# A tile's outputs and its state's products put side by side on TensorE, the state's products alternating between a head's halves

## The chip, the cores and the metric

The kernel runs on one NeuronCore of a Trainium2 chip. TensorE (PE, with its weight loads shown apart as PEld) multiplies, VectorE (DVE), ScalarE (ACT) and GpSimd (POOL) work on elements, SyncE (SP) issues most DMA transfers. Each engine takes its own instructions in order and waits for others at semaphores. Tiles lie in the on-chip memory of 128 partitions; TensorE's results go to banks of their own (PSUM), from where VectorE or ScalarE fetch them. The metric is the device time of one execution in microseconds; the median of three runs is given.

## The reference

A linear attention with a complex decay, for 4 batches, 8 heads, 768 steps and 48 columns a head, and then a mixture of 8 experts of which each token takes two:

```python
for t in range(S):
    new_re = ar * S_re - ai * S_im
    new_im = ar * S_im + ai * S_re
    S_re, S_im = (new_re + k_t (x) v_t, new_im)
    y[t] = q_t @ S_re
...
logits = x @ w_gate; noisy = logits + log1p(exp(x @ w_noise)) * noise
out[n] = sum over the best two e of weight * (relu(x @ w1[e]) @ w2[e])
```

Here `ar`, `ai` are the decay's two parts, scaled so that their size stays below 0.999, and x is y with the heads side by side (3072 tokens of 384).

## The kernel before

Attention is done in chunks of 128 steps: 6 groups of 4 tiles, tile n being batch n % 4 and group n // 4. The decay's running products are folded into q and k: `qh` and `kh` hold for each head two halves of 48 columns (the cosine and the sine part, at column 0 and 64). One tile then passes these steps:

- `tr_unit`: 8 transposes of `qh` and 8 of `kh` into the bank pair `ptr` (L298), which ScalarE copies to `qT` and `kT` (L299).
- `sc_unit`, twice, for 4 heads each: scores `psc` (L307), which VectorE multiplies by the causal mask into `am` (L308).
- `st_unit`: the state's products, for each head and each half `kh` times `v`, 48 by 48, into the bank `pG` (L317). The first halves go to partitions 0 to 47, the second to 64 to 111. The loop over the halves is the outer one: eight heads' first halves, then eight heads' second halves. The last group needs none.
- `st_upd`: VectorE adds `pG` to the batch's state `Z` (L326, or copies it in the first group, L329). `st_scale` multiplies `Z` by the chunk's decay (L338).
- `y_unit`: the outputs, 48 rows for each head, in the bank `pY`: `Z` times `qT` (L354, not in the first group) and `v` times `am` (L356), added up. Two heads share a column of the bank, one at partition 0, the other at 64, and the loop goes pair by pair, in turn between the two. ScalarE copies `pY` to `xT` (L357).
- `x_unit`, the gates (`gate_logits`, `gate_dispatch`) and the scatter to the experts' rows follow; part of the first expert's work (`mm1(0, 0)`, into `psc`) is mixed into the last groups.

Two buffers each hold `qh` and `kh` (`NQ` = 2), so that `kh` of tile n+2 (L288) waits until the transposes and the state's products of tile n have read it. `pG` and `pY` are single.

The order of the work is planned. Each step gets a due time from the table `P` by `at(...)`: scores at n - 0.2, state's products at n + 0.05, outputs at n + 0.2, the state's update at n + 0.4. The program is written in the order of these times, and a scheduler then places each instruction on its engine by its own estimate of when operands are ready, by the order of writing, and by a priority (`pri`) that some steps have. It may put instructions of other steps between those of one step. Of each matmul in float32 the trace shows two records.

Of the kernel before, what the change touches and what calls it, by code (L numbers as in the profile page):

```python
# [77 lines left out]
def kernel(  # L78
# [8 lines left out]
    nc = tc.nc  # L87
# [3 lines left out]
    D = HD // H  # L91
# [28 lines left out]
    mask = cp.tile([128, 128], F32, name="mask")  # L120
# [63 lines left out]
    pG = psA.tile([112, H, D], F32, name="pG", bufs=1)  # L184
# [2 lines left out]
    nc.vector.memset(pY, 0.0)  # L187


    RE, IM, T0, TH, TF, TR, EE, QK, V = {}, {}, {}, {}, {}, {}, {}, {}, {}  # L190
    QT, KT, AM, Z, XR, QKD = {}, {}, {}, {}, {}, {}
    XT, FC = {}, {}

    phases = {}

# [6 lines left out]
    def bt(n):  # L202
        return n % B, n // B
# [97 lines left out]
    def sc_unit(n, half):  # L301
        if half == 0:
            AM[n] = pa.tile([128, H, 128], F32, name="am", bufs=2)
        p = psA.tile([128, 4, 128], F32, name="psc")
        for j in range(4):
            h = 4 * half + j
            nc.tensor.matmul(p[:, j, :], KT[n][:, h, :], QT[n][:, h, :], start=True, stop=True)  # L307
        LAST['am'] = nc.vector.tensor_mul(AM[n][:, 4 * half:4 * half + 4, :], p, mask[:, None, :].to_broadcast([128, 4, 128]))  # L308

    def st_unit(n):  # L310
        b, g = bt(n)
        if g + 1 == NG:
            return
        x = kh[n % NQ]
        for r in range(2):
            for h in range(H):
                nc.tensor.matmul(pG[64 * r:64 * r + D, h, :], x[:, h, r, 0:D], V[n][:, h, :], start=True, stop=True)  # L317

    def st_upd(n):
        b, g = bt(n)  # L320
# [19 lines left out]
    def y_unit(n):  # L340

        b, g = bt(n)
        if b == 0:
            XR[g] = pa.tile([128, B, ROW], F32, name="xr", bufs=3)
            nc.gpsimd.memset(XR[g][:, :, RNO + 1:ROW], 0.0)
            nc.gpsimd.tensor_copy(XR[g][:, :, RNO], tokid[:, g])
        XT[n] = pa.tile([128, H // 2, 128], F32, name="xT", bufs=6)
        for i in range(H // 2):
            for z in range(0 if g else 1, 2):
                for r in range(2):  # L350
                    h = 2 * i + r
                    o = pY[64 * r:64 * r + D, i, :]
                    if z == 0:
                        nc.tensor.matmul(o, Z[b][:, h, :], QT[n][:, h, :], start=True, stop=False, skip_group_check=True)  # L354
                    else:
                        nc.tensor.matmul(o, V[n][:, h, :], AM[n][:, h, :], start=not g, stop=True, skip_group_check=True)  # L356
        LAST['y'] = YC[n] = nc.scalar.activation(XT[n], pY, AF.Copy)  # L357


# [75 lines left out]
    def at(step, f, *a):  # L435
        fill.setdefault(step, []).append((f, a))
# [42 lines left out]
        return psA.tile([128, 4, 128], F32, name="psc").rearrange("p a b -> p (a b)")  # L479


    order = mybir.DependencyInfo(mybir.DependencyClass.NoSync, mybir.DependencyReason.DATA)
    LAST = {}

    def behind_of(x, *names):
# [75 lines left out]
    def mm2(e, w):  # L561
        for j in JS[w]:
# [8 lines left out]
            else:  # L571
# [16 lines left out]
    P = dict(la=10, p1=7, d1=1, p2=6, dt=0, ds=0, lqk=6, p3=4, d3=0, q=2, lv=5, xu=0.5, ss=3, gl=0, gd=0.25,  # L588
             tr=1.4, sc=-0.2, st=0.05, y=0.2, up=0.4, w1=16.5, w2=21.1, xt=17.8, m1=18.4, dm=0.36, xu1=22.8, w1b=23, co=6, hg=50,
             hx=50, hl=200, s0=(7, 5.5, 4.5), s1=(7.5, 6, 5), qd=0.05, tk=0.4, sh=0.05)  # L590
    pri = {gdis: P["hg"], x_unit: P["hx"], glog: P["hl"]}
    for g in range(NG):
        f = B * g + .5
        q1, q2, q3 = P.get(f"s{g}", (P["p1"], P["p2"], P["p3"]))
        for j in range(B // 2):
            m = B * g // 2 + j
# [5 lines left out]
        for j in range(B):  # L602
            n = B * g + j
# [5 lines left out]
    for n in range(NT):  # L609
        at(n + .5 - P["lv"], load_v, n)  # L610
        for i in range(2):
            at(n - P["tr"] + P["tk"] * i, tr_unit, n, i)
        for half in range(2):
            at(n + P["sc"] + P["sh"] * half, sc_unit, n, half)
        at(n + P["st"], st_unit, n)
        at(n + P["y"], y_unit, n)
        at(n + P["up"], st_upd, n)
        at(n + .5 + P["xu"], x_unit, n)
        at(n + .5 + P["ss"], st_scale, n)
# [287 lines left out]
```

## Time and profile before

| what | us |
|---|---|
| three runs, median (lowest to highest) | 734.89 (734.31 to 736.23) |
| the profiled execution's span; the page gives no other time of it | 734.8 |
| TensorE, matmuls busy | 696.3 (95%) |
| TensorE, weight loads busy | 620.1 (84%) |
| VectorE busy | 418.7 (57%) |
| ScalarE busy | 329.8 (45%) |
| GpSimd busy | 170.4 (23%) |
| state's products `pG` (L317), 640 records | 31.2, mean 0.210 |
| outputs `pY` (L354 and L356), 704 records | 38.6 + 44.4, mean 0.276 and 0.275 |
| scores `psc` (L307), 384 records | 52.2, mean 0.281 |
| mean granted TensorE clock | 0.993 |

Matmuls overlap in TensorE: a record lasts from its issue until its last result, and the next one starts long before. The time that a series takes is therefore read from the starts, not from the sum of the records. A timeline row holds one or more records of a line that follow each other: start of the first, time until the end of the last, engine, line, operands and count; in brackets the idle time ahead and what ended it.

### The profile page before, as it was taken

To read this page: it belongs to the slowest core of one execution; us is meant where nothing else is said; L and a number is where in the kernel's file an instruction comes from. 1 tells how busy PE (TensorE), PEld (TensorE's weight loads), DVE (VectorE), ACT (ScalarE), POOL (GpSimd) and SP (SyncE) were. 2 spreads that over 40 slices of the span, in tenths; PEclk is the share of its full clock that TensorE was granted. 3 is DMA by queue.
4 is the path that set the end of the run, shared out by engine and by line. 5 is a ranking of instruction groups with operands and counts; after the bars stand their busy time and mean duration, and the time that the engine had idled before them with its cause. 6 is when DMAs were issued, how large, how long until landed. Compare 5 with 4: busy or idle time off the path is not lost.

```text
span 734.8 us, 13448 instructions
## 1 busy us (share of the span) xinstructions
PE 696.3 (95%) x5184; PEld 620.1 (84%) x5184; DVE 418.7 (57%) x946; ACT 329.8 (45%) x545; POOL 170.4 (23%) x187
## 2 busy tenths in 40 slices
PE   1689999999999999999999999999999999999995
PEld 0377687979788979898998999899999899899895
DVE  6788899999987666445255236236227226325321
ACT  6689989797954541333143124125115205203200
POOL 2000003333311254114114124124023123222221
PEclk9989999999999999999999999999999999999998
DMA  7477776754373457126144036028017126212101
GB/s 262 109 240 224 245 205 204 218 163 110 113 204 110 153 169 265 62 93 208 56 160 162 25 121 228 22 75 281 11 65 258 44 68 230 76 37 62 51 28 38
DMA packets 64090, 100.18 MB, mean 136 GB/s; under 512 B 26290, under 2 KB 46363, under 8 KB 64016
## 3 DMA queue, kind: packets, MB, share of 16 engines
q1 hardware_dynamic: 54464, 71.68, 31.2%
q0 software_dynamic: 9552, 27.54, 10.6%
q8 instruction: 43, 0.70, 0.4%
q14 instruction: 31, 0.25, 0.1%
HBM read 68.55 MB, written 32.08 MB: 137 GB/s over the span
## 4 chain that ended last, share of the span: by engine, by line
PE 84%; ACT 5%; DVE 4%; DMA 4%; issue 1%; SPq 1%; POOL 0%; POOLq 0%; ACTq 0%; DVEq 0%
PE po L569 27%; PE ph L545 27%; PE ptr L298 5%; PE psc L307 4%; PE pG L317 3%; PE px L528 2%; PE pY L356 2%; PE cum L251 2%; PE pY L354 2%; PE cum L275 2%; DMA raw<-in_moe_w_dram 2%; PE po L574 2%; PE po L577 2%; PE cum L364 1%; ACT t L200 1%
## 5 line engine op out<-in xcount | busy, mean ns | idle before, releaser
L569 PE MATMUL po<-w2h,h 128*128 128x384 f32 x768 | 198.7, 336 | 0.0
L545 PE MATMUL ph<-x,w1h 128*128 128x512 f32 (+1 forms) x720 | 194.8, 355 | 0.5 <-DVE h L550 0.2
L545 PEld LDWEIGHTS ph<-x,w1h 128*128 128x128 f32 x720 | 127.8, 188 | 16.8 <-issue 0.8
L569 PEld LDWEIGHTS po<-w2h,h 128*128 128x128 f32 x768 | 138.8, 188 | 0.9
L569 PE MATMUL po<-w2l,h 128*128 128x384 f32 x384 | 129.0, 336 | 0.0
L545 PE MATMUL ph<-x,w1l 128*128 128x512 f32 (+1 forms) x360 | 127.6, 355 | 0.0
L550 DVE SCALAR_TENSOR_TENSOR h<-ph,h 128x512 fp32r<-128x512 f32 (+2 forms) x176 | 73.4, 452 | 89.0 <-ACT h L547 88.9
L583 POOL DMA_INDIRECT out_dram<-ao,ox x56 | 54.6, 975 | 287.8 <-DVE ao L582 266.4
L547 ACT ACTIVATE h<-ph 128x512 fp32r<-128x512 f32 (+1 forms) x120 | 61.1, 522 | 116.2 <-PE ph L545 98.0
L421 POOL DMA_INDIRECT xs<-xr,sl x48 | 57.9, 1207 | 208.4 <-ACT t L200 104.7
L582 DVE SCALAR_TENSOR_TENSOR ao<-po,gw,ao 128x384 f32<-128x384 f32 (+1 forms) x56 | 34.2, 613 | 121.0 <-PE po L569 120.9
L545 PEld LDWEIGHTS ph<-x,w1l 128*128 128x128 f32 x360 | 67.7, 188 | 7.9
L569 PEld LDWEIGHTS po<-w2l,h 128*128 128x128 f32 x384 | 72.1, 188 | 0.7
L490 ACT CAST w2h<-raw 128x768 fp32r<-128x768 f32 x32 | 26.7, 836 | 90.7 <-PE po L569 87.1
L556 POOL DMA_INDIRECT ao<-out_dram,ox x49 | 51.7, 1054 | 48.0 <-DMA out_dram<-ao,ox 35.2
L307 PE MATMUL psc<-qT,kT 112*128 112x128 f32 x384 | 52.2, 281 | 0.0
L307 PEld LDWEIGHTS psc<-qT,kT 112*128 112x128 f32 x384 | 48.0, 195 | 2.7 <-issue 1.2
L356 PE MATMUL pY<-am,v 128*48 128x128 f32 x384 | 44.4, 275 | 0.9 <-DVE am L308 0.8
L354 PE MATMUL pY<-qT,z 112*48 112x128 f32 x320 | 38.6, 276 | 0.8 <-ACT xT L357 0.8
L491 DVE TENSOR_TENSOR w2l<-raw,w2h 128x768 fp32r<-128x768 f32 x32 | 30.7, 958 | 13.1 <-ACT w2h L490 11.9
L580 ACT COPY lo<-po 64x384 f32<-64x384 f32 x8 | 3.8, 477 | 73.4 <-PE po L577 73.3
L298 PE MATMUL ptr<-ident,qh 128*112 128x128 f32 x192 | 29.3, 284 | 7.4 <-ACT kT L299 6.7
(209 smaller groups left out, 1010.8 us busy)
## 6 DMA issues: line engine op xcount, KB each, us to landing
raw<-in_moe_w_dram SPq DMA_DIRECT2D x24, 512.0 KB, 4.4
raw<-in_moe_w_dram SPq DMA_DIRECT2D x32, 384.0 KB, 4.1
qk<-in_qk_dram SPq DMA_DIRECT2D x24, 384.0 KB, 3.8
xgb<-xs SPq DMA_DIRECT2D x8, 800.0 KB, 6.2
re<-in_a_dram SPq DMA_DIRECT2D x12, 384.0 KB, 3.4
im<-in_a_dram SPq DMA_DIRECT2D x12, 384.0 KB, 5.5
v<-in_v_dram SPq DMA_DIRECT2D x24, 192.0 KB, 2.5
out_dram<-zero SPq DMA_DIRECT2D x12, 384.0 KB, 5.5
```

The costliest lines, as they stand in the source:

```text
L298: nc.tensor.transpose(p[:, h, :], x[:, h, :, :].rearrange("p r x -> p (r x)")[:, 0:112], ident)
L307: nc.tensor.matmul(p[:, j, :], KT[n][:, h, :], QT[n][:, h, :], start=True, stop=True)
L354: nc.tensor.matmul(o, Z[b][:, h, :], QT[n][:, h, :], start=True, stop=False, skip_group_check=True)
L356: nc.tensor.matmul(o, V[n][:, h, :], AM[n][:, h, :], start=not g, stop=True, skip_group_check=True)
L421: d = nc.gpsimd.indirect_dma_start(out=xs, out_offset=bass.IndirectOffsetOnAxis(ap=sl[:, kk, b:b + 1], axis=0), in_=XR[g][:, lo + b, :], i ...
L545: LAST['m'] = nc.tensor.matmul(p[:, :n], W1[e, kk][i][:, f * 128:(f + 1) * 128], XW[w, kk][:, j, :], start=(m == 0), stop=(m == len(ms) - 1))
L547: nc.scalar.activation(h[:, 0:n], p[:, :n], AF.Relu)
L550: LAST['h'] = nc.vector.scalar_tensor_tensor(h[:, dst:dst + b - a], p[:, a:b], 0.0, h[:, a:b].bitcast(F32), op0=OP.max, op1=OP.subtract)
L556: nc.gpsimd.indirect_dma_start(out=ao[j][0:w, :], out_offset=None, in_=out, in_offset=bass.IndirectOffsetOnAxis(ap=OX[e][0:w, j:j + 1], ax ...
L569: nc.tensor.matmul(p[:, :DM], HT[w, f][i][:, o:o + 128], W2[f // 2][k2][:, f % 2, :], start=(m == 0), stop=(m == len(ms) - 1))
L582: nc.vector.scalar_tensor_tensor(a, p[0:n, :DM], g, a, op0=OP.mult, op1=OP.add)
L583: nc.gpsimd.indirect_dma_start(out=out, out_offset=bass.IndirectOffsetOnAxis(ap=OX[e][0:n, j:j + 1], axis=0), in_=a, in_offset=None, bound ...
```

## The change

In `st_unit` the loops change places: each head's first half is followed by its second. The scheduler gets a high priority (300) for `st_unit` and `y_unit`, and the due time of `st_unit` is now that of `y_unit`, written behind it. Two dependencies are added. The first matmul of the outputs waits for the second half of `am` (with a semaphore, `whole`); before, each waited for the half that it reads, and those that read `Z` for none. The first of the state's products is ordered behind the last of the outputs (`order`, on the same engine and so without a semaphore). What is computed stays the same.

```diff
     def st_unit(n):
         ...
-        for r in range(2):
-            for h in range(H):
-                nc.tensor.matmul(pG[64 * r:64 * r + D, h, :], x[:, h, r, 0:D], V[n][:, h, :], start=True, stop=True)
+        for h in range(H):
+            for r in range(2):
+                m = nc.tensor.matmul(pG[64 * r:64 * r + D, h, :], x[:, h, r, 0:D], V[n][:, h, :], start=True, stop=True)
+                if h + r == 0:
+                    tc.add_manual_dep(m.ins, YL[n].ins.name, order, reason="order")
...
+                    if not started:
+                        tc.add_manual_dep(m.ins, AMD[n].ins.name, whole, reason="whole")
+                    started = True
+        YL[n] = m
...
-    pri = {gdis: P["hg"], x_unit: P["hx"], glog: P["hl"]}
+    pri = {gdis: P["hg"], x_unit: P["hx"], glog: P["hl"], st_unit: 300, y_unit: 300}
...
-        at(n + P["st"], st_unit, n)
         at(n + P["y"], y_unit, n)
+        at(n + P["y"], st_unit, n)
```

TensorE before, tile 7 (`kh_127`, `z_775`; a row is one or more equal instructions, output, inputs, shape of the output), from the last of its scores on:

```order
L307 MATMUL psc<-qT,kT 128x128
L317 MATMUL pG<-v,kh_127 48x48 x2
L364 MATMUL cum<-ident,xT 128x128 x4
L317 MATMUL pG<-v,kh_127 48x48 x2
L298 MATMUL ptr<-ident,kh_126 112x128 x8
L317 MATMUL pG<-v,kh_127 48x48 x12
L354 MATMUL pY<-qT,z_775 48x128 x2
L356 MATMUL pY<-am,v 48x128 x2
```

The same place with the change (lines after the new code have higher numbers: L310 is the scores, L301 the transposes, L374 those of `x_unit`, L360 and L362 the outputs, L320 the state's products):

```order
L301 MATMUL ptr<-ident,qh_124 112x128 x2
L310 MATMUL psc<-qT,kT 128x128 x2
L374 MATMUL cum<-ident,xT 128x128 x4
L310 MATMUL psc<-qT,kT 128x128 x6
L360 MATMUL pY<-qT,z_775 48x128 x2
L362 MATMUL pY<-am,v 48x128 x2
```

The outputs now stand directly behind the tile's last scores, and the 16 state's products follow the last of the outputs in one row; the transposes of the next `kh` have moved behind them.

TensorE before, tile 11, from the end of its outputs on:

```order
L354 MATMUL pY<-qT,z_775 48x128 x2
L356 MATMUL pY<-am,v 48x128
L251 MATMUL cum<-t_1637,tri_t 128x384 x2
L356 MATMUL pY<-am,v 48x128
L298 MATMUL ptr<-ident,qh_125 112x128 x6
```

And with the change, where L254 is the former L251:

```order
L360 MATMUL pY<-qT,z_775 48x128 x2
L362 MATMUL pY<-am,v 48x128 x2
L320 MATMUL pG<-v,kh_127 48x48 x16
L254 MATMUL cum<-t_1733,tri_t 128x384 x2
L301 MATMUL ptr<-ident,kh_126 112x128 x6
```

The decay's matmuls no longer cut the last pair of outputs in two. Over the whole program the outputs and state's products stand in 49 unbroken series before and in 24, one for each tile, with the change; from tile 4's outputs on it is 40 and 20.

VectorE around the state's update and the next `kh`, in the group of tiles 8 to 11, before:

```order
L308 TENSOR_TENSOR am<-psc,mask 128x512 x2
L288 TENSOR_TENSOR qh_124<-qk,tr 128x2x8x48
L338 TENSOR_TENSOR z_555<-z_555,fcol 112x384
L326 TENSOR_TENSOR z_482<-z_482,pG 112x384
L288 TENSOR_TENSOR kh_126<-qk,tr 128x2x8x48
```

With the change (L311 is the mask, L283 the product of q and k with the decay, L331 the update of `Z`, L291 the former L288):

```order
L311 TENSOR_TENSOR am<-psc,mask 128x512 x2
L283 TENSOR_TENSOR qk<-qk,ee 128x768
L331 TENSOR_TENSOR z_482<-z_482,pG 112x384
L283 TENSOR_TENSOR qk<-qk,ee 128x768
L291 TENSOR_TENSOR kh_126<-qk,tr 128x2x8x48
```

Update and `kh` still wait for the tile's state's products; other multiplications now stand ahead of both.

More of the change, by code (lines that the diff above doesn't have):

```diff
@@ L187 @@
     nc.vector.memset(pY, 0.0)
+    order = mybir.DependencyInfo(mybir.DependencyClass.NoSync, mybir.DependencyReason.DATA)
+    whole = mybir.DependencyInfo(mybir.DependencyClass.Sync, mybir.DependencyReason.SCHED_ONLY)
     RE, IM, T0, TH, TF, TR, EE, QK, V = {}, {}, {}, {}, {}, {}, {}, {}, {}
@@ L192 @@
     XT, FC = {}, {}
+    AMD, YL = {}, {}
     phases = {}
@@ L307, in sc_unit @@
             nc.tensor.matmul(p[:, j, :], KT[n][:, h, :], QT[n][:, h, :], start=True, stop=True)
-        LAST['am'] = nc.vector.tensor_mul(AM[n][:, 4 * half:4 * half + 4, :], p, mask[:, None, :].to_broadcast([128, 4, 128]))
+        LAST['am'] = AMD[n] = nc.vector.tensor_mul(AM[n][:, 4 * half:4 * half + 4, :], p, mask[:, None, :].to_broadcast([128, 4, 128]))
     def st_unit(n):
@@ L347, in y_unit @@
         XT[n] = pa.tile([128, H // 2, 128], F32, name="xT", bufs=6)
+        started = False
         for i in range(H // 2):
@@ L353, in y_unit @@
                     if z == 0:
-                        nc.tensor.matmul(o, Z[b][:, h, :], QT[n][:, h, :], start=True, stop=False, skip_group_check=True)
+                        m = nc.tensor.matmul(o, Z[b][:, h, :], QT[n][:, h, :], start=True, stop=False, skip_group_check=True)
                     else:
-                        nc.tensor.matmul(o, V[n][:, h, :], AM[n][:, h, :], start=not g, stop=True, skip_group_check=True)
+                        m = nc.tensor.matmul(o, V[n][:, h, :], AM[n][:, h, :], start=not g, stop=True, skip_group_check=True)
+                    if not started:
+                        tc.add_manual_dep(m.ins, AMD[n].ins.name, whole, reason="whole")
+                    started = True
+        YL[n] = m
         LAST['y'] = YC[n] = nc.scalar.activation(XT[n], pY, AF.Copy)
@@ L479, in ps_tile @@
         return psA.tile([128, 4, 128], F32, name="psc").rearrange("p a b -> p (a b)")
-    order = mybir.DependencyInfo(mybir.DependencyClass.NoSync, mybir.DependencyReason.DATA)
     LAST = {}
```

## The prediction

> **What bounds the kernel now.** I read the page's slices and chain of waits first, then the engines' busy time in stretches of the attention stage.
>
> ```profile
> span 734.8 us, 13448 instructions
> PE   1689999999999999999999999999999999999995
> PE 84%; ACT 5%; DVE 4%; DMA 4%; issue 1%; SPq 1%; POOL 0%; POOLq 0%; ACTq 0%; DVEq 0%
> ```
>
> TensorE is full from the fourth slice on and holds 84% of the chain. The experts' matmuls are not touched, so everything is decided in the attention stage, up to some 270 us. Its stretches (from and to in us, length, then busy us and count of PE, PEld, DVE, ACT, POOL):
>
> ```profile
> 25.00:50.00 25.00, 16.91 (x177) 14.06 (x177) 22.62 (x33) 20.27 (x28) 0.00 (x0) 0.86 0.72 222
> 50.00:75.00 25.00, 24.19 (x239) 19.93 (x239) 21.41 (x32) 24.43 (x37) 0.00 (x0) 1.00 0.64 192
> 99.90:137.50 37.60, 37.60 (x464) 32.36 (x463) 35.66 (x85) 32.15 (x52) 9.31 (x5) 1.00 0.68 208
> 137.50:174.26 36.76, 36.76 (x464) 32.04 (x463) 34.55 (x84) 31.12 (x51) 13.82 (x13) 1.00 0.55 168
> 174.26:214.06 39.80, 39.34 (x486) 33.35 (x486) 36.45 (x111) 28.33 (x46) 11.09 (x15) 1.00 0.42 131
> 214.06:240.00 25.94, 25.94 (x284) 21.98 (x284) 20.29 (x66) 12.47 (x24) 3.62 (x4) 1.00 0.47 156
> ```
>
> Before 77 us TensorE often waits for others. From 99.9 to 214.06 (twelve tiles, 114.2 us) it is full, and VectorE is busy for 35.66 + 34.55 + 36.45 = 106.7 of them: 7.5 us are free there. After 214 VectorE has room. TensorE time saved from 77 us on is therefore worth its length, until VectorE's 7.5 us in the middle are used up.
>
> **Alternating the halves.** First a tile whose block has nothing between (tile 17), then its state's products pG in three small windows (a row there: start of the first record in flight, time to the last one's end):
>
> ```profile
> 202.69 1.73 PE L307 MATMUL psc<-qT,kT 112*128 112x128 f32 x14
> 204.25 1.04 PE L298 MATMUL ptr<-ident,kh 128*112 128x128 f32 x8
> 205.22 1.36 PE L317 MATMUL pG<-v,kh 128*48 128x48 f32 x29
> 206.38 0.31 PE L354 MATMUL pY<-qT,z 112*48 112x128 f32 x1
> 206.42 0.30 PE L317 MATMUL pG<-v,kh 128*48 128x48 f32 x3
> 208.07 0.41 PE L356 MATMUL pY<-am,v 128*48 128x128 f32 x3
> 208.41 1.09 PE L298 MATMUL ptr<-ident,qh 128*112 128x128 f32 x8
> ...
> 205.30 0.48 PE L317 MATMUL pG<-v,kh 128*48 128x48 f32 x7
> 205.66 0.48 PE L317 MATMUL pG<-v,kh 128*48 128x48 f32 x10
> 206.02 0.43 PE L317 MATMUL pG<-v,kh 128*48 128x48 f32 x6
> 106.32 0.24 PE L405 MATMUL cum<-ohs,ones_b 128*128 128x8 bf16 x4
> ```
>
> How long one record lasts is the mean in the groups by shape:
>
> ```profile
> L307 PE MATMUL psc<-qT,kT 112*128 112x128 f32 x384 | 52.2, 281 | 0.0
> L356 PE MATMUL pY<-am,v 128*48 128x128 f32 x384 | 44.4, 275 | 0.9 <-DVE am L308 0.8
> L317 PE MATMUL pG<-v,kh 128*48 128x48 f32 x640 | 31.2, 210 | 0.0
> L298 PE MATMUL ptr<-ident,kh 128*112 128x128 f32 x192 | 25.8, 274 | 0.1
> L405 PE MATMUL cum<-ohs,ones_b 128*128 128x8 bf16 x54 | 3.0, 166 | 0.0
> ```
>
> A product is two records, and a pG record lasts 0.21. Inside one half they start every (0.48 - 0.21)/6 = 45 ns, and the same in the other half ((0.43 - 0.21)/5 = 44). In the middle window, where the halves meet, ten records start within 0.27 us, 30 ns apart on average: the second half runs beside the rest of the first. The outputs pY, which alternate already, say the same: 32 records start from 206.38 to 208.07 + 0.41 - 0.27 = 208.21, every 59 ns, while a psc record of the same 128 columns takes (1.73 - 0.28)/13 = 112 ns. The pG block takes 1.29 us now (205.22 to 206.42 + 0.30 - 0.21). With the halves side by side it takes 16 x 45 ns = 0.72; the shortest step between records in this trace, (0.24 - 0.17)/3 = 25 ns in the L405 row, would make it 0.80. That saves 0.49 to 0.57, and I take 0.50. Fifteen tiles (5 to 19) have their pG after 77 us: **-7.5 us** (bounds -7.3 to -8.5).
>
> The Trainium skill ("TensorE: Matmul & The Clock Gate", Part 3, The mechanism) says that a weight load overlaps running matmuls only where its row group differs, and both halves here use the same 128 rows. By that rule this term would be nothing; the middle window speaks against it. It is rival B.
>
> **One block per tile.** Entering a block costs a step of 205.22 - (204.25 + 1.04 - 0.27) = 0.20 us in place of (1.04 - 0.27)/7 = 0.11; leaving it again 0.20 (208.21 to 208.41), and the next step is some 0.05 longer. Together 0.23 per visit. Where an output is cut off, its last pair pays more:
>
> ```profile
> 148.30 0.30 PE L354 MATMUL pY<-qT,z 112*48 112x128 f32 x2
> 148.72 1.56 PE L251 MATMUL cum<-t,tri_t 128*128 128x384 f32 x4
> 150.21 0.42 PE L356 MATMUL pY<-am,v 128*48 128x128 f32 x2
> 150.56 0.87 PE L298 MATMUL ptr<-ident,qh 128*112 128x128 f32 x6
> ...
> 76.70 0.43 PE L354 MATMUL pY<-qT,z 112*48 112x128 f32 x4 [0.83 <-ACT xT L357]
> 264.79 0.42 PE L354 MATMUL pY<-qT,z 112*48 112x128 f32 x4
> ```
>
> Here two records hold TensorE from 150.21 to 150.56, 0.35 us in place of 0.11 in the stream, with 0.09 ahead: 0.33. From 76.70 to 264.79 the trace has 40 such visits (first and last quoted); the new order has 20, one for each of tiles 4 to 23. Twenty fewer at 0.25, nearer to the plain case: **-5.0 us** (-4.6 to -6.6). Six of the twenty lie before 99.9, nine in the middle, five after; with one, twelve and two pG, both terms free 2.0, 8.25 and 2.25 us there.
>
> **The wait for the whole of `am`.** Before, pG or the Z part of pY ran while VectorE masked the scores; now the first pY matmul waits for both halves, and TensorE's queue behind it with it: pG, the next transposes and scores, so ACT's copies and VectorE's next mask as well. How late is `am` (L308)? Tiles 6 and 7, the least and (with tile 14) the most late, after their last scores:
>
> ```profile
> 97.32 1.79 PE psc L307 x16
> 99.14 0.69 DVE L308 TENSOR_TENSOR am<-psc,mask 128x512 f32<-128x512 f32 x1
> ...
> 106.42 0.47 PE L307 MATMUL psc<-qT,kT 112*128 112x128 f32 x2
> 109.45 0.68 DVE L308 TENSOR_TENSOR am<-psc,mask 128x512 f32<-128x512 f32 x1
> ```
>
> The second half ends at 99.83, 0.72 after the scores' end (99.11), and at 110.13, 3.24 after (106.89); the mean over tiles 6 to 17 is 1.4. In the new order there stand between scores and pY: nothing in tile 7; some 0.87 us in tiles 9, 12, 13, 16 and 17 (eight transpositions of 0.11, or two and one matmul of the decay, L251 or L275: four records of two such matmuls take from 148.72 to 148.72 + 1.56 - 0.27, 0.64 each); 1.3 to 1.7 in the others. The stall is lateness + 0.14 - cover: 0.14 because TensorE is free 0.08 before its last record ends, and I allow 0.06 for the signal. Were VectorE always as prompt as in tile 6, the stalls of tiles 4 to 23 would add up to some 1.5 us; as late as it was in each tile, some 10. I take **+4.5**, nearer the low end, since the two great delays (tiles 7 and 14) came with VectorE work of the gates and the decay in front, which TensorE itself now meets later in its own queue. Twelve of the twenty tiles, so 2.7 of the 4.5, lie in the middle: 8.25 - 2.7 = 5.5 us of gain there, inside VectorE's 7.5 but close enough that I don't go lower.
>
> **What moves later.** pG now ends some 2.5 us after the block's start, not 1.3; the state's update of Z and the next but one `kh`, which reuses its buffer, wait for it on VectorE:
>
> ```profile
> DVE kh L288 <- PE pG L317: 2.3, 4, 1.1
> 168.93 0.96 DVE L288 TENSOR_TENSOR kh<-qk,tr 128x768 f32<-128x768 f32 x1 [0.32 <-PE pG L317]
> 173.46 0.88 PE ptr L298 x8
> ```
>
> Tile 15's `kh` ends at 169.89 and is transposed from about 173.46 (the chain's row): 3.5 us of slack cover the 1.2 us for TensorE, and the new order puts other multiplications of VectorE between mask and `kh`. I take 0 (rival A gives the price if not). The pG of tiles 0 to 4 stood in time when TensorE waited anyway; tile 4's now falls after 77 us, and tile 2's `kh` can come only after the first block: **+0.7** (0 to 1.5; 0.7 is one block). The line of DMA issues is unchanged but for its times.
>
> **Sum**: -7.5 - 5.0 + 4.5 + 0.7 = -7.3 us. The profiled execution's span is 734.8 and the page gives no other time of it; the three runs' median is 734.89, 0.1 off. 734.8 - 7.3 = **727.5 us**. After 264 us nothing I see fixes the end by the clock: the hand-over waits for ScalarE's and VectorE's splits and the last gates, which follow the attention stage.
>
> **Rivals.**
>
> A. *VectorE waits for the later pG* (slower). If each `kh` or Z update of the twelve middle tiles waited the whole 1.2 us longer, VectorE would need 106.7 + 2.3 + 14.4 = 123.4 us for a stretch of 114.2: +9.2 there; with -4.25 in the other stretches and +0.7 that is 740.5. It decides once the mean wait passes 7.5/12 = 0.6 us per tile. For it: VectorE is the next fullest, and `kh` waited for pG four times already. Against: 3.5 us of slack.
>
> B. *The halves do not run side by side.* -5.0 + 4.5 + 0.7 = +0.2: 735.0, no change. Against: the middle window and the pY steps.
>
> C. *VectorE stays as late as it was*: stalls of 10 us eat the gain, -12.5 + 10 + 0.7 = -1.8: 733.0, no change that can be told. For it: VectorE at 93% in the middle, tile 7's 3.24 us. Against: its order has moved with TensorE's.
>
> D. *Hardly any stall*: -12.5 + 1.5 + 0.7 = -10.3: 724.5. For it: where VectorE is prompt, 0.88 us of transpositions cover 0.72 + 0.14, and five more tiles have 1.3 or more.
>
> **How the numbers follow.** Forecast 0.48, D 0.17, C 0.18, B 0.07, A 0.10. A measurement of this kernel can tell 0.3%, 2.2 us, from no change. The forecast (-4 to -9, 726 to 731) and D are faster; of C and B, whose times are not exact either, I count 0.06 as faster by more than 2.2 us and 0.01 as slower. Faster 0.71, same 0.18, slower 0.11. Range 722.5 to 737: from about both terms at their high ends with the low stall (-8.5 - 6.6 + 1.5 + 0.7 = -12.9, 721.9, all at once being unlikely) to B with the early cost and a pair of tiles' stalls at their bounds (735.0 + 0.8 + 1.2); A's 740.5 is left out. The forecast's own range is 726 to 731.
>
> **What would show it.** Right: a pG group of all 32 records in a row of about 0.95 us (0.72 + 0.21) in place of 1.36 + 0.30; 20 visits from tile 4 on, each with about 2.5 us from first to last start where it was 2.99; TensorE idle ahead of pY put down to `am`, 1.5 to 8 us in sum; the last pY some 7 us before 264.79. The alternation is wrong if pG records start 45 ns apart over the whole block; the visits, if leaving a block costs less than 0.2; the wait, if idle ahead of pY is above 10 us; A, if VectorE's waits for pG pass 7 us in the middle. The whole is wrong if the last pY comes early and the experts start no earlier.

## The result and the profile after

The changed kernel takes 745.46 us (median of four runs, 741.26 to 747.45); the kernel before, beside it, 735.02 (734.31 to 736.23). The ratio is 1.0128, with a 95% interval of 1.0095 to 1.016: **slower**, by 9.4 us as the ratio has it (the two medians lie 10.4 apart), where 727.5 was predicted. The profiled execution took 745.58 us. Its page, with the span, the slices of TensorE and its granted clock:

```profile
span 743.9 us, 13438 instructions
PE   1487989898979998999999999999999999999995
PEclk9899999999998999999999999999999999999998
```

Before, TensorE's row is all nines from the fourth slice to the last but one. Now it is torn through the whole attention stage (a slice is 18.6 us), and the experts' part behind it is as full as it was. So the loss lies where the change was made, though not in the matmuls that it touched. Those did what was forecast. TensorE around the block of tile 17, the timeline:

```profile
206.90 1.04 PE L301 MATMUL ptr<-ident,kh 128*112 128x128 f32 x8
207.92 0.42 PE L360 MATMUL pY<-qT,z 112*48 112x128 f32 x4
...
209.50 0.39 PE L362 MATMUL pY<-am,v 128*48 128x128 f32 x4
209.72 0.89 PE L320 MATMUL pG<-v,kh 128*48 128x48 f32 x32
```

All 32 records of pG stand in one row of 0.89 us, where they took 1.36 and 0.30 in two; from first to last start they take 0.89 - 0.21 = 0.68 us, which was 1.29. The whole block takes 209.72 + 0.68 - 207.92 = 2.48.

For the rest I cut the attention stage where ScalarE starts to copy a tile's outputs (`xT`): tile 4 to tile 17, 17 to 18, and 18 to 22. Busy time by stretch (length, then PE, PEld, DVE, ACT and POOL with their counts, granted clock, DMA share, GB/s), before:

```profile
83.14:208.52 125.38, 125.36 (x1535) 106.27 (x1534) 114.83 (x271) 103.82 (x171) 33.69 (x30) 1.00 0.55 168
208.52:217.36 8.84, 8.38 (x119) 7.84 (x120) 7.98 (x37) 4.75 (x8) 1.96 (x2) 1.00 0.81 234
217.36:261.21 43.85, 43.74 (x431) 38.18 (x432) 29.33 (x95) 22.90 (x41) 6.68 (x6) 1.00 0.43 149
```

and after:

```profile
83.37:209.94 126.57, 116.02 (x1521) 99.22 (x1518) 112.35 (x269) 103.07 (x170) 39.34 (x30) 1.00 0.54 164
209.94:227.71 17.77, 12.32 (x135) 11.25 (x131) 12.15 (x41) 7.23 (x10) 2.14 (x2) 0.81 0.71 215
227.71:268.84 41.13, 40.88 (x452) 36.94 (x449) 27.66 (x91) 20.43 (x38) 7.27 (x6) 1.00 0.35 119
```

In the **middle** TensorE has 125.36 - 116.02 = 9.34 us less to do, and stands idle for 126.57 - 116.02 = 10.55, where it was idle for 0.02: the whole gain is gone, and 1.2 us more. VectorE is not full either: it is idle for 14.2 us, more than before (10.5). From tile 17 to 18 the change **loses 8.9 us at one place**. Behind it 2.7 us are gained. These three sum to +7.4, and the span's +9.1 has the rest before tile 4 (0.2) and behind tile 22 (1.5).

What TensorE waits for in the middle, the waits from 84 to 209 us (engine, line, releaser: sum in us, times, longest), with VectorE's longest:

```profile
PE cum L254 <- DVE t L249: 2.9, 2, 1.6
PE ptr L301 <- ACT kT L302: 2.6, 3, 1.1
PE pY L360 <- DVE am L311: 1.9, 3, 0.8
PE ptr L301 <- DVE ga4oh L61: 1.8, 1, 1.8
DVE qk L283 <- ACT ee L203: 11.6, 8, 2.9
```

In the kernel before the same view has no wait of TensorE, and of VectorE for the exponentials `ee`:

```profile
DVE qk L280 <- ACT ee L200: 0.6, 2, 0.4
```

Only 1.9 of 10.5 us are the wait for `am` that the change wrote down. The others are between instructions that the diff doesn't name: 2.9 for the decay's carry `t`, 2.6 for the copies `kT` of transposed k, and 1.8 that the view puts down to the gates' `ga4oh`. That last one is the longest single wait of the middle, and the rows around it say what it was for:

```profile
176.02 0.94 DVE L291 TENSOR_TENSOR kh<-qk,tr 128x768 f32<-128x768 f32 x1
176.89 0.21 DVE L61 TENSOR_TENSOR ga4oh<-iota,ga4ix 128x64 f32<-128x64 f32 x1
177.11 1.06 PE L301 MATMUL ptr<-ident,kh 128*112 128x128 f32 x8 [1.83 <-DVE ga4oh L61]
```

TensorE starts the transposes of tile 15's `kh` here (the sixteenth `kh` of VectorE, since tiles count from 0). They read `kh` and not `ga4oh`, and `kh` was finished 0.15 us before, so I read this as a wait for `kh`. In the kernel before, the same `kh` was done 3.4 us before its transposes.

The instructions stand in another order because the scheduler fills all queues anew around the new blocks. The tables by which kernels below hold the old and the new order list 317 instructions of ScalarE and 531 of VectorE, and at most 239 and 363 of them come in the same sequence in both.

The place between tile 17 and 18, ScalarE's timeline after:

```profile
216.96 1.04 ACT L499 CAST w1h<-raw 128x1024 fp32r<-128x1024 f32 x1 [2.05 <-DMA raw<-in_moe_w_dram]
219.07 1.04 ACT L499 CAST w1h<-raw 128x1024 fp32r<-128x1024 f32 x1 [1.07 <-DMA raw<-in_moe_w_dram]
220.02 1.02 ACT L302 ACTIVATE kT<-ptr 112x1024 f32<-112x1024 f32 x1
```

before:

```profile
214.17 1.02 ACT L299 ACTIVATE kT<-ptr 112x1024 f32<-112x1024 f32 x1 [1.29 <-PE ptr L298]
215.09 1.04 ACT L490 CAST w1h<-raw 128x1024 fp32r<-128x1024 f32 x1
```

and TensorE after:

```profile
215.47 1.04 PE L301 MATMUL ptr<-ident,kh 128*112 128x128 f32 x8
221.09 0.99 PE L537 MATMUL ptr<-ident,xga 128*128 128x128 f32 x3 [4.58 <-ACT kT L302]
222.01 2.07 PE L310 MATMUL psc<-qT,kT 112*128 112x128 f32 x8
224.01 0.67 PE L360 MATMUL pY<-qT,z 112*48 112x128 f32 x4
224.47 0.64 PE L362 MATMUL pY<-am,v 128*48 128x128 f32 x4
```

Two casts of the first expert's weights now stand ahead of tile 19's `kT` on ScalarE and wait there for their transfer. The transposes are done at 216.51, the copy starts at 220.02; TensorE waits 4.58 us, and tile 18's outputs stand behind in its queue. The Trainium skill ("TensorE: Matmul & The Clock Gate", Architectural detail) says that ScalarE and VectorE take their queue strictly in order, and this trace agrees. After the gap TensorE runs at half speed for a while: a row of four pY records takes 0.64 us where it took 0.39 at 209.50, and the next row starts some 0.43 us later where that was 0.22. The granted clock is 0.50 from 221.09 to 227.70, and 0.81 over the whole stretch.

### The profile page after: what moved, and what is told of

Read it like the earlier page. It is cut to its first block, busy times and chain, and to the rows that moved or that the text cites. A ratio compares the mean times of both kernels' runs of the same rounds, so it can differ in the third digit from the quotient of the medians.

```text
span 743.9 us, 13438 instructions
## 1 busy us (share of the span) xinstructions
PE 684.7 (92%) x5184; PEld 613.8 (83%) x5184; DVE 419.2 (56%) x946; ACT 329.4 (44%) x545; POOL 178.3 (24%) x187
## 4 chain that ended last, share of the span: by engine, by line
PE 59%; DMA 1%; DVE 1%; ACT 1%; issue 0%; POOL 0%; POOLq 0%; DVEq 0%
PE po L578 27%; PE ph L554 26%; PE px L537 2%; PE po L586 1%; PE po L583 1%; DMA raw<-in_moe_w_dram 1%; DVE w1l L500 0%; DMA xs<-xr,sl 0%; ACT w1h L499 0%; ACT w2h L499 0%; DVE ao L591 0%; PE cum L383 0%; DVE w2l L500 0%; POOL out_dram L592 0%; DVE x L542 0%
## 5 line engine op out<-in xcount | busy, mean ns | idle before, releaser
L431 POOL DMA_INDIRECT xs<-xr,sl x48 | 64.2, 1338 | 212.2 <-DVE am L311 120.2
L310 PE MATMUL psc<-qT,kT 112*128 112x128 f32 x384 | 51.8, 283 | 0.3 <-DVE h L559 0.3
L310 PEld LDWEIGHTS psc<-qT,kT 112*128 112x128 f32 x384 | 48.1, 198 | 2.3 <-issue 0.8
L301 PE MATMUL ptr<-ident,qh 128*112 128x128 f32 x192 | 29.1, 284 | 11.0 <-ACT kT L302 10.4
L362 PE MATMUL pY<-am,v 128*48 128x128 f32 x384 | 36.4, 279 | 2.2 <-DVE am L311 2.2
L500 DVE TENSOR_TENSOR w1l<-raw,w1h 128x1024 fp32r<-128x1024 f32 x24 | 29.3, 1224 | 12.0 <-ACT w1h L499 11.9
```

What stands on the lines that cost most here:

```text
L301: nc.tensor.transpose(p[:, h, :], x[:, h, :, :].rearrange("p r x -> p (r x)")[:, 0:112], ident)
L362: m = nc.tensor.matmul(o, V[n][:, h, :], AM[n][:, h, :], start=not g, stop=True, skip_group_check=True)
L431: d = nc.gpsimd.indirect_dma_start(out=xs, out_offset=bass.IndirectOffsetOnAxis(ap=sl[:, kk, b:b + 1], axis=0), in_=XR[g][:, lo + b, :], i ...
L500: d = nc.vector.tensor_tensor(lo, raw_t, hi.bitcast(F32), op=OP.subtract)
```

## The experiments

From the two traces I took **theory Q**: the matmuls did get cheaper, and the loss comes from the order that the scheduler gave to VectorE's and ScalarE's queues. Against it stood **J** (joining the blocks, with the wait for `am` and the later pG, holds TensorE up whatever the other queues do) and **C** (halves that run side by side slow TensorE elsewhere). When Q and J both proved too simple, **K** took their place: what costs is that pG stands behind pY, either because `kh` of the next tile but one then comes late (**K1**) or because TensorE has nothing left to run while `am`'s second half is made (**K2**); **E** is named where it is tested.

The changed kernel's dependencies leave the scheduler free, so an experiment that edits one line may move rows in every queue. Some of the kernels below therefore keep another kernel's order row for row, and the text says which; where that isn't said, the queues were filled anew. In all sets but the one of `control`, `pG_first`, `third_kh` and `qk_later`, the kernel before took some 10 us more than in the first measurement (745 us against 735; more on that at the end), so times are compared as ratios to the kernel before in the same set. The cause of the 10 us is not known, and the wait that goes with them is not equally long in all kernels, so small differences between ratios should not be leaned on. The expectations of `alt`, `no_alternation`, `join_pinned` and `cast_late` are in us against 735.0.

### The alternation alone, and taken out

`alt` is the kernel before with the loops of `st_unit` exchanged. VectorE's and ScalarE's rows are those of before.

```diff
-        for r in range(2):
-            for h in range(H):
+        for h in range(H):
+            for r in range(2):
                 nc.tensor.matmul(pG[64 * r:64 * r + D, h, :], x[:, h, r, 0:D], V[n][:, h, :], start=True, stop=True)
```

> The kernel before with the two loops of the state's products swapped and nothing else: the order on VectorE and ScalarE stays that of before row for row, and on TensorE only the rows inside a block of 16 state's products change. Theory Q (the products did get cheaper, and the loss comes from the order that the scheduler gave to VectorE's and ScalarE's queues): 15 blocks on the bound path save 0.5 us each, so 735.0 - 7.5 = 727.5, between 726 and 729.5. Rival J (putting the two blocks together costs the time, with its wait for both halves of am and its later pG): the same 727.5, since nothing is put together here. Rival C (halves that run side by side slow TensorE elsewhere, through its clock or its ports): no gain or a loss, 735 or more.

Measured: 0.994 (0.992 to 0.9959). A gain, but 4.5 us, not 7.5. Its middle:

```profile
82.58:205.06 122.48, 119.81 (x1535) 99.44 (x1534) 114.09 (x271) 103.57 (x171) 30.96 (x30) 1.00 0.57 171
```

TensorE has 5.55 us less to do there and 2.67 of them turn into waits (1.2 for the carry and 1.0 for the gates are the largest), though no queue but its own changed. From first to last start an uncut pG block takes 0.72 us now, for 1.29, as forecast; yet TensorE is freed of only 5.55 / 13 = 0.43 us a tile. In the old order the outputs had already begun when the last pG records started (206.38 and 206.42 in the prediction's rows), so part of the 0.57 was in use before. The experiments' rival C is out, and so is rival B of the prediction.

`no_alternation` is the reverse: the changed kernel with the old loops, every other queue as in the changed kernel.

```diff
-        for h in range(H):
-            for r in range(2):
+        for r in range(2):
+            for h in range(H):
                 m = nc.tensor.matmul(pG[64 * r:64 * r + D, h, :], x[:, h, r, 0:D], V[n][:, h, :], start=True, stop=True)
```

> The changed kernel with the state's products in the old order of halves (all eight heads of one half, then of the other); the order on VectorE and ScalarE stays that of the changed kernel row for row. Theory Q: each of 20 blocks takes 0.5 to 0.6 us more on TensorE; where the queues' waits already hold TensorE up, part of it is hidden, so 745.5 + 4 to 10: 749 to 755. Rival J: the same. Rival C: the alternation is what costs, so it falls back to 733 to 740.

Measured: 1.0223 (1.018 to 1.0266), 1% above the changed kernel's 1.0128, or 7 us, as theory Q said (749 to 755 is 1.019 to 1.027 of 735).

```profile
85.47:217.35 131.88, 123.39 (x1528) 106.54 (x1527) 113.78 (x271) 103.84 (x169) 38.32 (x30) 1.00 0.53 157
```

With the blocks joined, this gives both TensorE terms their size in the middle's thirteen tiles: alternation 123.39 - 116.02 = 7.37 us, 0.57 a tile; fewer visits 125.36 - 123.39 = 1.97. Taken in the other order, by `alt`, the same 9.34 us split into 5.55 and 119.81 - 116.02 = 3.79. The sum is firm, the split depends on what the block has beside it.

### Holding queues in an old order

Three kernels held orders by a table of ranks, chained instruction by instruction with dependencies that set the order and wait for nothing:

```diff
+ORDER = {"DVE": "0+19 21 19 ...", "Activation": "...", "PE": "..."}
...
+        for x, y in zip(row, row[1:]):
+            tc.add_manual_dep(y, x.name, order, reason="order")
```

`join_pinned` has the whole change from tile 4 on, with VectorE, ScalarE and the rest of TensorE in the order of before; the joint block stands where pY began. (Tiles 0 to 3 can't all be joined in that order, since VectorE there takes pG of the first tiles into `Z` before it makes their `am`.)

> The whole change from tile 4 on (alternation, pG right behind pY, the wait for both halves of am), but with every other instruction of VectorE, ScalarE and TensorE held in the order that it has in the kernel before; the joint block stands where the first product of pY stood. Tiles 0 to 3 keep pG apart from pY. Theory Q: the two gains with hardly a wait, 735.0 - 7.5 - 16 x 0.25 = 723.5, plus 0 to 4 for waits for am, since the block now stands where pY began and am's second half may not be there: between 722 and 729. Rival J: the wait for am and the later pG cost what they cost in the changed kernel, so 740 to 747. Rival C: 740 or more as well; alt tells J and C apart.

`join_old_queues` leaves TensorE's order free:

> The whole change from tile 4 on, with VectorE's and ScalarE's instructions held in the order of the kernel before, and TensorE's order free, so that the joint block may stand where am is there (in join_pinned it stood where pY began, and TensorE waited 15 us for am). Theory Q: the gains without the waits, 0.985 to 0.998. Rival J: TensorE has nothing else to do while it waits for am's second half, and waits for later pG follow on VectorE: 1.010 to 1.028.

`old_blocks_new_queues` is the kernel before with VectorE's and ScalarE's order taken from the changed kernel:

> The kernel before (pG apart from pY, halves one after the other, no wait for both halves of am), with VectorE's and ScalarE's instructions held in the order that the changed kernel has; TensorE's order is free. Times as ratios to the kernel before, since chips differ. Theory Q (the loss comes from the order of VectorE's and ScalarE's queues): 1.013 to 1.030, since the waits of the changed kernel appear and nothing is saved on TensorE. Rival J (putting the blocks together holds TensorE up, whatever the other queues do): 0.997 to 1.008.

Measured: 1.028 (1.0248 to 1.0312), 1.0297 (1.0274 to 1.032) and 1.0303 (1.0262 to 1.0343). All three are worse than both kernels. The first lies above the ranges of Q and J, the second just above J's; the third lies at the upper end of Q's range, far above J's. TensorE's longest waits from tile 4 to tile 17 in `join_pinned`:

```profile
PE pY L407 <- DVE am L357: 10.7, 10, 2.9
```

in `join_old_queues`:

```profile
PE pY L392 <- DVE am L343: 5.7, 5, 1.7
PE ptr L333 <- ACT kT L334: 4.4, 4, 1.5
```

and in `old_blocks_new_queues`:

```profile
PE pY L388 <- DVE am L340: 4.3, 4, 2.0
```

Theory Q, as I had put it, falls on the first two: VectorE's and ScalarE's order of before does not rescue the joint blocks. The third bears its other half out, since the order of the changed kernel harms the old blocks too; but TensorE's own order was free there, and in the middle it has 130.42 us to do, 5 more than before, so not all of that loss is waiting. My reading is that neither order is bad in itself and that each fits the place of pG and pY for which it was made. With the old one the joint block comes when `am`'s second half isn't there: that wait is the first in both lists.

### One suspect at a time in the changed kernel

`cast_late` holds the three casts behind the copy of tile 19's `kT`:

```diff
+    for a in CAST[:3]:
+        tc.add_manual_dep(a.ins, TRC[1, 19].ins.name, order, reason="order")
```

> The changed kernel, with ScalarE's three casts of expert 0's first weights held behind the copy of tile 19's kT, as they stand in the kernel before; nothing else is held, so a few rows near that place move with it. Theory Q: the 4.6 us for which TensorE waits for that copy go, and with them the half clock that follows the idle time, 9 of the 10.5 us that the changed kernel loses: 745.5 - 9 = 736.5, between 734 and 740. Rivals J and C: nothing that they rest on is touched, 744 to 747.

Measured: 1.0081 (1.0055 to 1.0107): 0.47% or 3.5 us of the loss go, where Q said 9. The stretches behind tile 17:

```profile
210.32:220.52 10.20, 8.16 (x146) 7.80 (x144) 8.55 (x37) 5.67 (x9) 2.15 (x2) 1.00 0.69 180
220.52:265.23 44.71, 42.10 (x442) 37.62 (x438) 30.38 (x95) 21.86 (x41) 7.56 (x6) 1.00 0.44 153
```

7.6 us are saved at the place itself, the half clock with them, and 3.6 given back in the next stretch. There a cast waits for its transfer again, now ahead of the gates' copy `lt`, and TensorE with it:

```profile
223.66 1.04 ACT L499 CAST w1h<-raw 128x1024 fp32r<-128x1024 f32 x1 [2.55 <-DMA raw<-in_moe_w_dram]
225.24 0.30 PE L388 MATMUL cum<-ident,lt 96*128 96x96 f32 x1 [1.69 <-ACT lt L386]
```

`no_whole_wait` takes out the dependency on both halves of `am`, `no_priority` the priority of 300; both let the scheduler order everything anew.

```diff
                     if not started:
-                        tc.add_manual_dep(m.ins, AMD[n].ins.name, whole, reason="whole")
+                        pass
```

```diff
-    pri = {gdis: P["hg"], x_unit: P["hx"], glog: P["hl"], st_unit: 300, y_unit: 300}
+    pri = {gdis: P["hg"], x_unit: P["hx"], glog: P["hl"]}
```

> The changed kernel without the wait of a block's first product for both halves of am; pG still stands right behind pY, and the scheduler orders all queues anew. Theory Q: another order, good or bad by chance, 0.995 to 1.020, with stalls named by copies of kT and qT or by the decay's carry. Rival J: the wait for am is what holds TensorE up, so without it most of the loss goes: 0.985 to 0.997.

> The changed kernel without the priority of 300 for the two blocks; the joint block and the wait for am stay, and the scheduler orders all queues anew, with the block later in TensorE's queue. Theory Q: another order, good or bad by chance, 0.995 to 1.020. Rival J: the block is put behind more of TensorE's other work, so am is there when it comes: 0.990 to 1.003.

Measured: 1.0161 (1.0144 to 1.0178) and 1.0202 (1.0156 to 1.0247). Taking out either one does not take the loss away, and J's ranges are missed by both; with all queues filled anew this doesn't show that neither has a part in it. In `no_whole_wait` the waits for `am` are gone from TensorE's list, and `ptr` waits 6.6 us for `kT` in the middle.

`qk_later` moves the multiplications for which VectorE stood idle 11.6 us back in its queue:

```diff
+    for n in (12, 16, 20):
+        tc.add_manual_dep(QM[n].ins, PQ[n - 2, 1].ins.name, order, reason="order")
+    for n in (8, 9):
+        tc.add_manual_dep(QM[n].ins, AMD[5].ins.name, order, reason="order")
```

> The changed kernel with VectorE's multiplications of qk by the decay held back a few places in its queue in each group of tiles (tiles 8 and 9 behind the mask of tile 5; tiles 12, 16 and 20 behind kh of two tiles earlier). VectorE stands idle 11.6 us between 84 and 209 us in the changed kernel because these multiplications come ahead of ScalarE's exponentials; in the kernel before 0.6. Theory E (this idle time makes VectorE late, and with it am, kh and the carry, for which TensorE then waits): the wait of qk falls below 4 us, and 5 to 9 us of the loss go: 1.001 to 1.007. Theories K and Q: the waits of TensorE stay, 1.009 to 1.020.

Measured: 1.0167 (1.0134 to 1.02). VectorE's wait fell to 3.6 us as meant, and nothing was gained. So theory E finds no support: this idle time of VectorE goes with the new order, and taking most of it away did not bring the loss back.

### Why the joint block has nothing to fill the gap

In the changed kernel VectorE makes most `kh` right behind the update of `Z` from two tiles earlier: `kh` reuses a buffer that pG reads, pG now stands behind pY, and pY waits for both halves of `am`. In the middle's thirteen tiles `kh` of tile n+2 starts on average 4.9 us after the second mask of tile n does; before it was 3.4. `third_kh` gives `kh` a third buffer (and `xT` five for six); `pG_first` puts pG ahead of pY in the block, with pG waiting for the first half of `am` only:

```diff
-    kh = [pa.tile([128, H, 2, 64], F32, name=f"kh{i}") for i in range(NQ)]
+    kh = [pa.tile([128, H, 2, 64], F32, name=f"kh{i}") for i in range(NQ + 1)]
```

```diff
                 if h + r == 0:
-                    tc.add_manual_dep(m.ins, YL[n].ins.name, order, reason="order")
+                    tc.add_manual_dep(m.ins, AMH[n, 0].ins.name, whole, reason="whole")
+        YL[n] = m
...
                     if not started:
-                        tc.add_manual_dep(m.ins, AMD[n].ins.name, whole, reason="whole")
+                        if n in YL:
+                            tc.add_manual_dep(m.ins, YL[n].ins.name, order, reason="order")
+                        tc.add_manual_dep(m.ins, AMH[n, 1].ins.name, whole, reason="whole")
...
-        at(n + P["y"], y_unit, n)
         at(n + P["y"], st_unit, n)
+        at(n + P["y"], y_unit, n)
```

> The changed kernel with a third buffer for kh, so that kh of the next tile but one no longer waits for pG (room for it comes from xT, five buffers for six). Theory K: most of the loss goes, 0.985 to 1.002. Theory Q: 1.005 to 1.025, the waits only move to other places. A wait for xT's buffers, if the sixth was needed, would show by its name.

> The changed kernel with the two blocks the other way round: the state's products pG first, waiting for the first half of am alone, and the outputs pY right behind them, waiting for the second half. Still one visit per tile and halves alternating. Theory K (the loss comes from pG standing behind the wait for am, and with it kh of the next tile but one, which waits for pG's buffer): most of the loss goes, ratio 0.985 to 1.000, and the waits of ptr for the copies of kT fall below 2 us in the middle (7.1 in the changed kernel). Theory Q (any order but the fitted one costs): 1.008 to 1.025.

Measured: 1.0076 (1.0044 to 1.0109), in Q's range and not in K's, and 0.9973 (0.9955 to 0.9992), in K's. `third_kh` makes `kh` 3.0 us ahead of that mask on average. There the waits for `kT` have left TensorE's list of the middle and the mask is first in it:

```profile
PE pY L360 <- DVE am L311: 4.6, 5, 1.4
PE cum L254 <- DVE t L249: 3.0, 3, 1.1
```

The wait at tile 15's `kh` is gone too. So an early `kh` goes with no wait for `kT`, and most of what it frees comes back at `am`. In `pG_first` the loss is gone. The middle of `third_kh`, then the middle of `pG_first` and its stretch from tile 17 to 18:

```profile
84.33:207.99 123.66, 114.42 (x1504) 97.68 (x1504) 111.76 (x265) 100.30 (x165) 30.38 (x30) 1.00 0.55 166
83.48:203.20 119.72, 115.84 (x1522) 96.51 (x1523) 111.56 (x263) 99.75 (x165) 29.54 (x30) 1.00 0.57 171
203.20:212.39 9.19, 8.12 (x122) 7.50 (x123) 7.46 (x35) 4.71 (x8) 2.59 (x2) 1.00 0.81 224
```

In `third_kh` the middle is 2.9 us shorter than in the changed kernel, but TensorE's idle time there falls only from 10.55 to 9.24. In `pG_first` TensorE has as little to do as in the changed kernel (115.84 for 116.02) and stands idle 3.88 us in place of 10.55. More than that comes from the place between tiles 17 and 18: 9.19 us for 17.77. In 7 of the 20 tiles of `pG_first` that have a pG other matmuls stand between pG and pY. This kernel changed two things at once, so `pG_first_whole` lets pG too wait for both halves (`AMH[n, 1]` for `AMH[n, 0]`): against the changed kernel the two blocks are exchanged, still with no matmul between, and the wait is the same.

> The changed kernel with the two blocks the other way round and nothing else: pG waits for both halves of am, pY stands right behind it with no matmul between, in all 20 tiles. Against the changed kernel only the order inside the block differs, so the wait for am is the same, but kh of the next tile but one and the update of Z are free 1.5 us earlier. Theory K1 (the loss comes from pG behind pY, through kh): ratio 0.995 to 1.003, near pG_first (0.997). Theory K2 (the loss comes from having nothing left to run while the second half of am is masked): 1.006 to 1.016, and TensorE's waits for am in the middle stay at 2 to 6 us.

Measured: 1.0018 (1.0007 to 1.0028), in K1's range. Yet its trace does not bear K1's mechanism out in the middle:

```profile
85.95:211.71 125.76, 116.38 (x1531) 97.17 (x1531) 112.53 (x276) 98.37 (x164) 33.65 (x30) 1.00 0.53 160
211.71:219.48 7.77, 7.09 (x112) 6.52 (x111) 7.38 (x26) 4.42 (x8) 2.75 (x2) 1.00 0.88 253
```

```profile
PE pG L320 <- DVE am L311: 5.8, 5, 1.3
```

The middle is only 0.8 us shorter than in the changed kernel. The waits for `kT` are gone, as K1 says, and the wait for `am` has grown from 1.9 to 5.8 us, as K2 says (1.3 more, put down to the gates' `ga4e`, end 0.05 us after a mask does and belong to it as well). What it gains over the changed kernel lies between tiles 17 and 18 (7.77 us for 17.77), where one cast still stands ahead of the copy that TensorE needs, but finds its transfer done and doesn't wait. With pG let start after the first half, the wait for `am` is 1.3 us and the middle 119.72 for 125.76; the queues were filled anew for that, so the edit and the new order can't be told apart.

Three more kernels asked what is left in `pG_first`: the casts held back as in `cast_late`, a third `kh`, and the old order of halves with every queue as in `pG_first`.

> pG_first with ScalarE's three casts of expert 0's first weights held behind the copy of tile 19's kT. If the casts still cost something there (waits of 0.8 and 1.4 us near 215 us), 1 to 2 us are gained: 0.993 to 0.997. If not, 0.996 to 0.999, the same as pG_first.

> pG_first with a third buffer for kh (and five for xT). K1: kh is free early already, so little comes of it: 0.994 to 1.002. If the waits of ptr for copies of kT that are left in pG_first (1.5 us in the middle) come from kh's buffers, 0.990 to 0.995.

> pG_first with the state's products in the old order of halves; every queue keeps the order of pG_first row for row. TensorE has hardly a wait left there, so the alternation should show in full: 15 to 20 blocks at 0.50 us and the like, 7 to 10 us: ratio 0.997 + 0.010 to 0.014, so 1.007 to 1.011. If VectorE sets the pace in the middle once TensorE's work is shorter, less: 1.001 to 1.006.

Measured: 0.999 (0.9975 to 1.0005), 1.0111 (1.0094 to 1.0128) and 1.0066 (1.0049 to 1.0083). Holding the casts back gains nothing there. The third buffer, a help in the changed kernel, does harm here and misses both ranges: it, too, had all queues filled anew, and a middle of 131.64 us came out. In it `kh` comes earlier still (on average 6.1 us ahead of the mask), and in the middle TensorE still waits 4.9 us for `kT`, where `pG_first` has 1.5: an early `kh` alone does not take these waits away. Taking out the alternation costs 0.9%, some 7 us, as in `no_alternation`, and more than the 0.6% that `alt` gained by it.

### Side by side

`control` is the kernel before, for its trace.

> The kernel before, unchanged, for a trace on a chip where it takes 745 us. If the 10 us more are spread over the span (a slower clock, slower transfers), the tiles of the attention stage come some 1.3% later each; if they are one stall, the copy of tile 22's outputs by ScalarE starts at 261.2 us as in the first trace, and one wait of 5 to 8 us of ScalarE for something that the profile does not name follows it, as in the trace of alt (8.2 us).

It took 736.54 us in a set in which the kernel before took 735.66, with a span of 734.8 as in the first trace; the 10 us did not appear, so it tells nothing of them. Last, the two kernels that were faster than both given ones, on one chip:

> The same kernel as alt (the alternation alone, in the order of the kernel before), beside pG_first on one chip: ScalarE's copy of tile 22's outputs starts 3.8 us before that of the kernel before, and nothing is lost behind it if no unnamed wait of ScalarE falls there. 0.992 to 0.996.

> The same kernel as pG_first, beside alt_again: the copy of tile 22's outputs starts 4.5 to 5.4 us before that of the kernel before. If the whole gain arrives, 0.993 to 0.996, the same as alt; if part is lost behind the attention stage again, as its first timing says, 0.996 to 0.999.

Measured: 0.9941 (0.9927 to 0.9955) and 0.996 (0.9944 to 0.9976). The alternation alone is the fastest version measured, 0.6% ahead of the kernel before, though its interval overlaps that of `pG_first`; joining the blocks added nothing to it in any form tried.

## Why the prediction was wrong, by its own steps

- **What bounds the kernel.** "TensorE time saved from 77 us on is worth its length, until VectorE's 7.5 us are used up" did not hold. VectorE's free time was not used up, it grew (10.5 to 14.2 us in the middle), and `alt` lost 2.67 of 5.55 us to waits with not one row moved on another engine. A TensorE that is never idle does not show how close behind it the others run.
- **Alternating the halves**: right in its mechanism. 0.57 us a tile with the blocks joined, at the upper bound; 0.43 in `alt`, below the lower one, because the block's 1.29 us were counted to its last pG record although the outputs had begun before that. The rule of the Trainium skill ("TensorE: Matmul & The Clock Gate", Part 3, The mechanism) by which this term would be nothing disagrees with the trace: 32 records of two column halves over the same 128 rows start within 0.68 us.
- **One block per tile**: right in the main. 1.97 us in the thirteen tiles of the middle (3.79 by `alt`), where the nine visits that I counted for twelve of them make 2.25. Both terms together freed 9.34 us there, where 8.25 were forecast for twelve tiles.
- **The wait for the whole of `am`**: as a wait of TensorE, right and smaller than forecast (1.9 us in the middle, where 2.7 were said). But I took the stall for the whole price. Most of it stands in the other waits, as the next step says.
- **What moves later** is the step that failed, priced at 0 and +0.7. The note ahead of the prediction showed VectorE's new order, with other multiplications ahead of `kh`, and I called it cover because 3.5 us of slack stood in the old trace, behind tile 15's `kh`. That was one tile: tile 8's `kh` had only 0.9 us in the same trace. And slack read in the old order is not there in the new one: TensorE waits 1.83 us at this very `kh` of tile 15, the longest wait of the middle. What came in place of 0 and +0.7: 8.6 us of waits of TensorE in the middle other than for `am` (the carry 2.9, `kT` 2.6, tile 15's `kh` 1.8 and smaller ones), and 8.9 us between tiles 17 and 18, where the new order has casts that depend on a transfer ahead of a copy that TensorE needs. I had left the line of DMA issues as "unchanged but for its times", and the prediction shows no row of the experts' weights.
- **Rival A** had the right chain (pY, pG, `kh`) and the wrong engine: `kh` never waits for pG on VectorE in the new trace (from 77 us on, the only wait for pG is one of 1.7 us for `Z`). The new order puts `kh` late enough that it need not wait; that the delay then comes out as TensorE's waits, at tile 15's `kh` and for `kT`, is my reading of it.

What is shown: the sum of both gains, and the size of the alternation by kernels with all other queues equal; that the loss of the middle is idle TensorE time; that between tiles 17 and 18 the order of the casts costs most of the 8.9 us, since holding them back saves 7.6 there, though 3.6 come back in the next stretch; and that `pG_first`, whose block may begin with half of `am`, has 3.88 us of idle time in the middle where the changed kernel has 10.55. Argued, and not shown, is that a late `kh` is what makes the middle's waits: in the changed kernel a third buffer took away those for `kT`, in `pG_first` it brought more. What stays open: each kernel whose queues were filled anew got its own set of waits, with middles from 119.72 us (`pG_first`) to 131.64 (`pG_first_third_kh`), and I can't say how much of a single ratio belongs to its edit and how much to the order that came with it. Why the scheduler put the casts ahead of `kT`, I did not find out.

## What to carry to other kernels

Where a scheduler fills the queues, a new constraint on one engine can be paid on all of them: compare the order of every engine before pricing it, and look for three things in it, an instruction that waits for a transfer ahead of a copy that the bound engine needs, a buffer whose last reader has moved behind a wait, and work that used to fill a wait and is now chained to it. Read slack for every tile, not for one, and again in the new order. When a wait is put down to an instruction whose result the waiting one doesn't read, look at what it does read. If an edit has a part that leaves every order alone, try that part by itself: here it was worth 0.6%, and all of it was lost in the part that came along. When two blocks must stand together, try the one that needs less first and let it start on what is there; here that form lost nothing, where the other lost 1.3%.

## What the runs showed of the hardware

- Products that go in turn to two column halves of TensorE, 128 rows each, run side by side: the 32 records start within 0.68 us, in pairs some 6 ns apart with a pair every 45 ns, and 45 ns is the step that one half alone had. The 25 ns that I had taken from this kernel's shortest rows as a bound (0.80 us a block) is no bound for records in different halves.
- A gap of 4.58 us was followed by 6.6 us at half the clock (granted 0.50), with rows of four records of 0.64 us for 0.39. The Trainium skill ("TensorE: Matmul & The Clock Gate", Part 1, What's actually happening) has the clock halved after an idle window of some 3.4 us; the trace agrees.
- In the sets where the kernel before took 745 us, ScalarE stood still near the end of the attention stage, in ten of fourteen traces for 5.9 to 8.9 us with nothing in the profile that released it (in the other four the wait at the same place is 3.2 to 6.7 us and is put down to a matmul of the gates). `alt`:

```profile
262.10 0.22 ACT L200 ACTIVATE ga3w<-ga3u 128x24 f32<-128x24 f32 x1 [1.06 <-DVE ga3c L41]
270.55 0.60 ACT L357 ACTIVATE xT<-pY 128x512 f32<-128x512 f32 x1 [8.22 <-remote]
```

  The copy waits for pY alone, which was done by 263. The same copy in `alt_again` waited 8.76 us, and in no trace of the set in which the kernel before took 736 us is there such a wait, though `alt` and that set ran on the same chip. I did not find its cause. No trace of the kernel before in a set of 745 us is on record, so how much of the 10 us this wait makes up is not shown.
